# Weight sums of the odd blocks made in the last product's stage from raw weights, and a later place for one x group

## The chip, the cores and the metric

One core of one Trainium2 chip. The metric is the device time of one execution in microseconds (us); lower is better. The engines are named as in the profile: PE multiplies matrices (PEld is its weight load), DVE works elementwise with two inputs, ACT elementwise with one input and with activation functions, POOL and SP here mostly start DMAs. A chunk of a matrix is 128 wide.

## The reference, cut to what matters

```python
# x: 1 x 2048 x 640, w_gate and w_up: 640 x 1728, w_down: 1728 x 640
g = sigmoid((x * gate_w).sum(-1, keepdims=True))
a = dft_seq_re @ (x @ dft_hid_re.T) - dft_seq_im @ (x @ dft_hid_im.T)
b = (gelu(x @ w_gate) * (x @ w_up)) @ w_down
out = g * a + (1 - g) * b
```

All arrays are float32. 1728 is 13 chunks of 128 and 64 columns over.

## The kernel before, in words

**Number format.** Every float32 operand is split into a high part (line 80, a copy by ACT into the short type that PE reads fast) and a low part (line 83, raw minus high, by DVE). A product of two operands is three matmuls (lines 99 to 101): high by high, low by high, high by low. So every operand costs one ACT and one DVE instruction before PE may use it.

**Fewer products.** Blocks are multiplied two by two with the Winograd form of Strassen's scheme, seven block products in place of eight. It needs sums of blocks on both sides: for weights with blocks A11, A12, A21, A22 these are S1 = A21 + A22, S2 = S1 - A11, S3 = A11 - A21 and S4 = A12 - S2 (each with its own signs in the code).

**The stages, in time.** First products (to about 50 us). The gate and up stage, chunks f = 1 to 12, to about 335 us: `gate_up` for both halves of x, in which every second chunk from 3 on (kind 1) also has `together` and `together_up`, products shared by two chunks. Then the last product's stage, the product with w_down (about 335 to 502 us): 28 steps, `kseq`, 14 for each half tp. Then the C stage (the sequence transform, to about 895 us) and the last stage.

**What sets the order.** In the gate and up stage the order of PE, ACT, DVE and POOL is written out by hand (`in_order`, line 104). Side work stands in a list `fills`, each piece with an estimated cost, and is spread between the products of a chunk (line 1170); `left_work` is work for the leftover 64 columns, which is done either at once or where `spare` stands in the list of the next chunk's weights (line 236). `LEFT_AT` (line 690) says in which chunk which leftover work is entered; `store_left` (line 693) stores its results by SP at the start of the next chunk. In the last product's stage the order of ACT and DVE is written out (line 1277), that of SP and POOL is the tile framework's. In step i, `load_k(i + 3)` starts loads, `split_k(i + 2)` makes high and low parts, `late` does what is left over from an earlier step, and `step_k(i)` gives the products to PE.

**Buffers.** Nearly all tiles of 4 KB a partition share one pool of 46 slots, tag "s4" (line 63); a new tile waits until a slot is free. Tiles of 2 KB share 14 slots, tag "m".

**The steps of the last product.** For each half: steps (b = 0, k = 0 to 5) with the blocks A11, A12, e5 and S4; then the left block (b = 0, k = NK = 6), which joins the first chunk of w_down (`wd0`) with the 64 rows over (`wdr`); then (b = 1, k = 0), (b = 1, NK), which uses the left block's S2, S1, S3 and A22, and (b = 1, k = 1 to 5). So the left block is step 6 of the first half and step 20 of the second, and the step that uses its sums is 8 or 22. For each chunk k the weight sums are made beforehand in the gate and up stage and kept in DRAM as `wsd`; those of the left block are kept as `wsl`.

**sum_left (line 623).** In chunk 10 it loads A11 and A21 (`lw`), the narrow rows twice (`lm`) and the upper rows of the first chunk twice (`ld`), makes six sums on DVE (lines 637 to 645) and stores them into `wsl` (eight blocks, two stores). `load_k` for the left block then loads them beside the raw weights (lines 828 to 833), and `split_k` (lines 877 to 888) makes high and low parts of all blocks at once: `kc` and `ka` of the narrow ones, `kh` and `kl` of the wide ones.

**x groups (load_xn, line 757).** Eight groups of x for the C stage. Four of them are loaded, summed and split during the last product's stage, in the steps that `XN_AT` names: 1, 7, 18 and 24. A group takes seven slots, of which four stay until the end of the C stage.

**xq and xz.** In chunks of kind 1 after the third, POOL loads `xq` (line 1165), operands of `together`, and SP loads two `xz` tiles (line 746), whose row sums (line 750, DVE) make the gate g.

Of the kernel before, what the change touches and what calls it, by code (L numbers as in the profile page):

```python
# [22 lines left out]
NF = F // P  # L23
FR = F - NF * P
NK = (NF - 1) // 2
XN_AT = [1, 7, 18, 24]
GM_AT = [2, 17]
EORD = [0, 2, 1, 3, 4]
PAIRED = 3
# [6 lines left out]
def kernel(  # L36
# [27 lines left out]
    nc = tc.nc  # L64
# [14 lines left out]
    def high(hi, raw):  # L79
        nc.scalar.activation(hi, raw, AF.Copy)  # L80

    def low(hi, lo, raw):
        nc.vector.tensor_tensor(lo, raw, hi.bitcast(F32), op=ALU.subtract)  # L83

    def split(hi, lo, raw):
        high(hi, raw)
        low(hi, lo, raw)
# [37 lines left out]
    h0 = [dram.tile([P, 4, T], F32, tag=f"h0{p}", name=f"h0{p}") for p in range(2)]  # L125
    wsu, wneg = ([dram.tile([P, 8, P], F32, tag=f"{n}{p}", name=f"{n}{p}") for p in range(ND)] for n in ("wsu", "wneg"))
    uA, uT = ([[dram.tile([P, 4, T], F32, tag=f"u{n}{j}{p}", name=f"u{n}{j}{p}") for p in range(ND)] for j in range(2)] for n in "AT")
    grd, gmd = ([dram.tile([1, 2 * T], F32, tag=f"{n}{p}", name=f"{n}{p}") for p in range(2)] for n in ("grd", "gmd"))
    wsl = dram.tile([P, 8, P], F32, tag="wsl", name="wsl")
# [11 lines left out]
    def at(hilo, i):  # L141
        h, l = hilo
        return h[:, i], l[:, i]
# [6 lines left out]
    tt = nc.vector.tensor_tensor  # L150
# [82 lines left out]
    late_work, left_work, left_out = [], [], []  # L233
# [383 lines left out]

        return [(0, load), (84, do), (84, do)]

    def chunks(name):  # L620
        return mtile(F32, name).rearrange("p (b c) -> p b c", c=P)

    def sum_left():


        w, m, d = chunks("lw"), chunks("lm"), chunks("ld")
        nc.sync.dma_start(w, wd0[:, :4])
        for q in range(2):
            rows = slice(q * FR, (q + 1) * FR)
            nc.sync.dma_start(m[rows], wdr[:, :4])  # L630
            nc.sync.dma_start(d[rows], wd0[:FR, :4])
        a11, a21, a22 = w[:, 0:2], w[:, 2:4], m[:, 2:4]
        own = {}

        def first():
            s = own["s"] = chunks("ls")
            tt(s[:, 0:2], a21, a11, op=ALU.subtract)
            tt(a21[:FR], a21[:FR], a22[:FR], op=ALU.add)
            tt(m[:, 0:2], m[:, 0:2], a22, op=ALU.subtract)

        def second():
            s = own["s"]
            tt(a11, a11, a21, op=ALU.subtract)
            tt(d[:, 0:2], d[:, 0:2], d[:, 2:4], op=ALU.subtract)
            tt(s[:, 2:4], m[:, 0:2], d[:, 0:2], op=ALU.add)
            left_out.append((wsl[:, 0:4], w))
            left_out.append((wsl[:, 4:8], s))

        return [(100, first), (100, second)]

    def sum_h0(tp):


        f1, f2, b22 = (mtile(F32, f"lf{tp}{k}") for k in range(3))
        for v, k in ((f1, 0), (f2, 1), (b22, 3)):
            nc.sync.dma_start(v, h0[tp][:, k])

        def first():
            tt(f1, f2, f1, op=ALU.subtract)
            for k in (0, 2):  # L660
                rows = slice(FR if k else 0, P)
# [25 lines left out]

        return [(122, first), (61, second)]

    LEFT_AT = {2: lambda: [*sum_h0(0), *sum_h0(1)], 6: partial(sum_h0_narrow, 0), 10: sum_left, 11: lambda: [], 12: partial(sum_h0_narrow, 1)}  # L690


    def store_left():
# [120 lines left out]
    kraw, ktile = {}, {}  # L814

    def load_k(i):


        tp, b, k = kseq[i]
        n = f"{tp}{b}{k}"  # L820
        r = None
        if not (k == NK and b):
            r = slot(F32, [P, 8, P], f"kw{n}")
        if k == NK and b:
            src = hL[tp]
        elif k == NK:
            m = slot(F32, [P, 8, P], f"km{n}")
            nc.sync.dma_start(r[:, 0:2], wd0[:, 0:2])
            nc.sync.dma_start(r[:, 2:8], wsl[:, 0:6])
            for q in range(2):  # L830
                nc.sync.dma_start(m[q * FR : (q + 1) * FR, :5], wdr)
            nc.sync.dma_start(m[:, 5:7], wsl[:, 6:8])
            nc.sync.dma_start(m[:, 7], wd0[:, 4])
            r, src = (r, m), h0[tp]
        elif b:
            nc.sync.dma_start(r[:, 0:2], wd[k, :, 6:8])
# [33 lines left out]
    def split_k(i):  # L870
        tp, b, k = kseq[i]
        n = f"{tp}{b}{k}"
        r, raw = kraw.pop(i)
        if k == NK and b:
            W = ktile.pop(("left", tp))
        elif k == NK:
            r, m = r
            c, a = slot(F32R, [P, 8, P], f"kc{n}"), slot(F32R, [P, 8, P], f"ka{n}")
            high(c, m)
            high(a[:FR, :7], m[:FR, :7])  # L880
            low(c[FR:, :7], a[FR:, :7], m[FR:, :7])
            low(c[:, 7], a[:, 7], m[:, 7])
            h, l = slot(F32R, [P, 8, P], f"kh{n}"), slot(F32R, [P, 8, P], f"kl{n}")
            split(h, l, r)
            W = {name: (at((h, l), 2 * q), at((h, l), 2 * q + 1)) for q, name in enumerate(("A11", "S2", "S1", "S3"))}
            mx = {"A12": (a[:, 0], a[:, 1]), "A22": (a[:, 2], a[:, 3]), "e5": a[:, 4], "S4": (a[:, 5], a[:, 6])}
            W = W, (c[:, 7], a[:, 7]), mx
            ktile["left", tp] = W
        else:
            h, l = slot(F32R, [P, 8, P], f"kh{n}"), slot(F32R, [P, 8, P], f"kl{n}")  # L890
            split(h, l, r)
            names = ("A22", "S1", "S2", "S3") if b else ("A11", "A12", "e5", "S4")
            W = {name: (at((h, l), 2 * q), at((h, l), 2 * q + 1)) for q, name in enumerate(names)}
        B = []
        for q in range(2):
            v = hl(f"kb{n}{q}")
            split(*v, raw[q])
            B += [at(v, 0), at(v, 1)]
        ktile[i] = W, B

    kb = {"alone": False}
    after = []

    def late():
        for do in after:
            do()
        after.clear()
# [123 lines left out]
    with in_order(ACT, DVE, PE):  # L1031
# [5 lines left out]
        for d in range(ND):  # L1037
# [3 lines left out]
            if d == 0:  # L1041
                a, b = halves
# [56 lines left out]
        W, work = make_w(1)  # L1099
# [93 lines left out]
    with in_order(PE, ACT, DVE, POOL):  # L1193
        for f in range(1, NF):
# [80 lines left out]
            W = nxt  # L1275
# [5 lines left out]
    for i in range(len(kseq)):  # L1281
        if i + 3 < len(kseq):
            load_k(i + 3)
        if i + 2 < len(kseq):
            split_k(i + 2)
        late()
        if i in GM_AT:
            gm[GM_AT.index(i)] = gate_tile(gmd, GM_AT.index(i), f"gm{i}")
        if i in XN_AT:
            load_xn(XN_AT.index(i))  # L1290
        m = i - (len(kseq) - 3)
        if m >= 0:
# [12 lines left out]
        while todo:  # L1305
            todo.popleft()[1]()
# [50 lines left out]
    for i, (j, ri, b, sp) in enumerate(cseq):  # L1357
# [21 lines left out]
        if not b:  # L1379
# [17 lines left out]
            if lst:  # L1397
# [4 lines left out]
                for d in range(2):  # L1402
                    c = sv["c11", d]
# [5 lines left out]
        else:  # L1409
# [21 lines left out]
            if lst:  # L1431
                for d in range(2):
                    s2 = copy(X[d], f"s2{n}{d}")
                    a = mtile(F32, f"sa{n}{d}")
# [4 lines left out]
                for d in range(2):  # L1439
                    a, c21 = sv["a", d], mtile(F32, f"c21{n}{d}")  # L1440
# [3 lines left out]
                for d in range(2):  # L1444
                    s2, a, r, c12 = sv["s2", d], sv["a", d], sv["r", d], sv["c12", d]
# [41 lines left out]
    for i, (tp, b, p) in enumerate(useq[: 3 * ND]):  # L1487
        n = f"{tp}{b}"
        m = i - 2 * ND
# [20 lines left out]
        if not b:  # L1510
            for q in range(2):
                sv["c11", q] = copy(X[q], f"ys{n}{q}")
            for q in range(2):
                c = sv["c11", q]
# [3 lines left out]
            ls = [copy(L[t], f"yl{n}{t}") for t in range(2)]  # L1518
# [12 lines left out]
        for q in range(2):  # L1531
            s2, a = es[q]
# [159 lines left out]
```

## Time and profile before

| | |
|---|---|
| three runs | 1022.97 us median, 1022.27 to 1024.85 |
| profiled execution | 1022.46 us, of which the span from the first to the last instruction is 1020.5 |
| granted TensorE clock | 1.0 in every slice |
| DMA | 269.15 MB, 264 GB/s on average |

A view of waits has, in each row, the engine, the tile and line that waited, what it waited for, and the total, number and longest of these waits in us. A timeline row has start, duration, engine, line, operation, output <- inputs and shape, and in brackets the idle time before it and what seems to have ended it. "L83" is line 83, which may be a helper's. Where a wait is for several things, the row names the one that came last by the profile. Matmuls are pipelined: each is shown as 0.39 us long, although one starts every 0.23 us.

### The profile page before, as it was taken

Reading aid. Unit: us, or ns where it says so; the run is one execution under the profiler, and the core shown is the slowest. Engines: PE = TensorE matmul, PEld = TensorE weight load, DVE = VectorE, ACT = ScalarE, POOL = GpSimd, SP = SyncE. Lnnn points to the kernel's source line nnn. Section 1 sums busy time; section 2 is a strip of 40 time slices with the busy share of each in tenths; the row PEclk is TensorE's granted clock in tenths of the full one; section 3 lists DMA queues with packets and bytes.
Section 4 is the critical chain, followed back from the end, with each engine's and each line's share of the span. In section 5 each row is a group of like instructions: output and inputs, shape, how many; then the busy total and the mean of one; then the engine's idle time right before and its main releaser. Section 6 shows DMA issues by size and latency. Waiting matters only on the chain.

```text
span 1020.5 us, 13286 instructions
## 1 busy us (share of the span) xinstructions
PE 1015.2 (99%) x4483; PEld 839.0 (82%) x4483; DVE 823.9 (81%) x1163; ACT 485.9 (48%) x635; POOL 166.9 (16%) x295
## 2 busy tenths in 40 slices
PE   9999999999999999999999999999999999999998
PEld 7888888888878888888888888888888888888887
DVE  6987877877778979987898975898588859797796
ACT  6544534353535577366455343444344444465340
POOL 0121242323231200100011022102210200021112
PEclk9999999999999999999999999999999999999999
DMA  7468588968799999969776778658965877897855
GB/s 270 168 216 269 182 273 275 313 224 289 229 326 312 409 344 373 349 259 351 261 235 193 247 264 310 220 190 295 300 208 208 297 252 269 329 317 221 260 152 92
DMA packets 98084, 269.15 MB, mean 264 GB/s; under 512 B 12832, under 2 KB 28064, under 8 KB 98016
## 3 DMA queue, kind: packets, MB, share of 16 engines
q1 hardware_dynamic: 72096, 186.94, 53.6%
q0 software_dynamic: 25776, 81.30, 24.4%
q8 instruction: 35, 0.57, 0.2%
q14 instruction: 33, 0.27, 0.1%
q10 hardware_dynamic: 144, 0.07, 0.0%
HBM read 193.53 MB, written 70.80 MB: 259 GB/s over the span
## 4 chain that ended last, share of the span: by engine, by line
PE 98%; DMA 1%; DVE 1%; issue 0%; POOL 0%; SPq 0%; ACT 0%; POOLq 0%
PE pX L101 7%; PE pX L99 7%; PE pX L100 7%; PE pZ L101 4%; PE pZ L99 4%; PE pZ L100 4%; PE pL L101 3%; PE pL L99 3%; PE pL L100 3%; PE pV L101 2%; PE pV L99 2%; PE pV L100 2%; PE pY L101 1%; PE pR L101 1%; PE pQ L101 1%; PE pY L100 1%
## 5 line engine op out<-in xcount | busy, mean ns | idle before, releaser
L80 ACT ACTIVATE ch<-csa 128x1024 fp32r<-128x1024 f32 x32 | 34.0, 1064 | 89.5 <-DVE csa L797 70.6
L83 DVE TENSOR_TENSOR cl<-cra,ch 128x1024 fp32r<-128x1024 f32 x32 | 39.1, 1222 | 22.8 <-ACT ch L80 22.6
L80 ACT ACTIVATE ch<-cra 128x1024 fp32r<-128x1024 f32 x32 | 33.9, 1059 | 45.5 <-PE pL L100 15.6
L83 DVE TENSOR_TENSOR cl<-crb,ch 128x1024 fp32r<-128x1024 f32 x32 | 39.1, 1222 | 17.3 <-ACT ch L80 17.3
L100 PE MATMUL pL<-cl,xah 128*128 128x512 f32 x128 | 49.8, 389 | 0.0
L101 PE MATMUL pL<-ch,xal 128*128 128x512 f32 x128 | 49.8, 389 | 0.0
L99 PE MATMUL pL<-ch,xah 128*128 128x512 f32 x128 | 49.3, 389 | 0.0
L403 POOL DMA_DIRECT2D hA<-s x48 | 26.1, 544 | 131.5 <-DVE s L561 111.9
L80 ACT ACTIVATE ch<-crb 128x1024 fp32r<-128x1024 f32 x32 | 33.8, 1055 | 27.7 <-DVE cl L83 11.1
L83 DVE TENSOR_TENSOR cl<-csb,ch 128x1024 fp32r<-128x1024 f32 x32 | 39.2, 1224 | 4.5 <-ACT ch L80 2.3
L83 DVE TENSOR_TENSOR cl<-csa,ch 128x1024 fp32r<-128x1024 f32 x32 | 39.1, 1222 | 2.9 <-PE pR L100 1.7
L80 ACT ACTIVATE ch<-csb 128x1024 fp32r<-128x1024 f32 x32 | 34.0, 1062 | 12.5 <-PE pR L101 4.5
L555 ACT ACTIVATE s<-s 128x512 f32<-128x512 f32 x24 | 15.2, 634 | 47.0 <-DVE s L554 47.0
L83 DVE TENSOR_TENSOR kl<-kw,kh 128x1024 fp32r<-128x1024 f32 x26 | 31.7, 1220 | 6.9 <-ACT kh L80 6.9
L550 DVE TENSOR_TENSOR s<-s,pX 128x512 f32<-128x512 f32 x24 | 16.4, 684 | 19.8 <-PE pX L101 14.5
L1353 POOL DMA_DIRECT2D uA<-c x8 | 4.3, 540 | 169.8 <-DVE c L1441 169.6
L934 POOL DMA_DIRECT2D out<-ks x12 | 6.5, 542 | 154.2 <-DVE ks L933 153.6
L147 ACT ACTIVATE s<-pX 128x512 f32<-128x512 f32 x40 | 23.2, 597 | 15.5 <-PE pX L101 14.4
L403 POOL DMA_DIRECT2D hT<-s x48 | 26.0, 541 | 24.1 <-DVE s L578 8.1
L80 ACT ACTIVATE kh<-kw 128x1024 fp32r<-128x1024 f32 x26 | 27.2, 1048 | 2.0 <-DMA kw<-wsd 2.0
L100 PEld LDWEIGHTS pL<-cl,xah 128*128 128x128 f32 x128 | 24.0, 188 | 5.0
L101 PEld LDWEIGHTS pL<-ch,xal 128*128 128x128 f32 x128 | 24.0, 188 | 5.0
(3612 smaller groups left out, 3474.0 us busy)
## 6 DMA issues: line engine op xcount, KB each, us to landing
cra<-in_ct SPq DMA_DIRECT2D x64, 512.0 KB, 4.1
crb<-in_ct SPq DMA_DIRECT2D x64, 512.0 KB, 5.0
hA<-s POOLq DMA_DIRECT2D x48, 256.0 KB, 5.8
hT<-s POOLq DMA_DIRECT2D x48, 256.0 KB, 6.0
kr<-hA SPq DMA_DIRECT2D x24, 512.0 KB, 6.8
kr<-hT SPq DMA_DIRECT2D x24, 512.0 KB, 7.8
ux<-uA SPq DMA_DIRECT2D x24, 512.0 KB, 5.9
ux<-uT SPq DMA_DIRECT2D x16, 512.0 KB, 5.5
```

The lines of the kernel that those rows point to most:

```text
L80: nc.scalar.activation(hi, raw, AF.Copy)
L83: nc.vector.tensor_tensor(lo, raw, hi.bitcast(F32), op=ALU.subtract)
L99: nc.tensor.matmul(ps, lh, rh, start=first, stop=False, skip_group_check=True)
L100: nc.tensor.matmul(ps, lh, rl, start=False, stop=False, skip_group_check=True)
L101: nc.tensor.matmul(ps, ll, rh, start=False, stop=last, skip_group_check=True)
L147: nc.scalar.activation(m, src, AF.Copy)
L403: nc.gpsimd.dma_start(to[:, i], src)
L550: tt(s5, s5, X, op=ALU.add)
L555: nc.scalar.activation(s2, s2, AF.Gelu_apprx_tanh)
L934: nc.gpsimd.dma_start(acc4[:, t] if tp and e == 4 else out[2 * tp + t, e], src)
L1353: nc.gpsimd.dma_start(to[:, i], src)
```

## The change

`sum_left`, its helper `chunks`, the DRAM tile `wsl` and the entries 10 and 11 of `LEFT_AT` go. The left block's weights are now loaded raw in `load_k`, in both halves: `wd0` whole into `r`, the narrow rows `wdr` twice into `m`, and the upper rows of `wd0` twice into a new tile `d`. `split_k` makes the sums that the b = 0 step and the narrow products need (three on DVE), and splits only A11 and e5 of the wide blocks. A new function `split_left`, called one step later (steps 5 and 19) behind `split_k` and `late`, makes S2, S1 and S3 in place in `r` (three sums) and splits seven blocks at once. The tiles `r` and `m` live until then. The third x group moves from step 18 to step 21.

```diff
-XN_AT = [1, 7, 18, 24]
+XN_AT = [1, 7, 21, 24]
...
-    def sum_left():
...
-    LEFT_AT = {2: lambda: [*sum_h0(0), *sum_h0(1)], 6: partial(sum_h0_narrow, 0), 10: sum_left, 11: lambda: [], 12: partial(sum_h0_narrow, 1)}
+    LEFT_AT = {2: lambda: [*sum_h0(0), *sum_h0(1)], 6: partial(sum_h0_narrow, 0), 12: partial(sum_h0_narrow, 1)}
...
             m = slot(F32, [P, 8, P], f"km{n}")
-            nc.sync.dma_start(r[:, 0:2], wd0[:, 0:2])
-            nc.sync.dma_start(r[:, 2:8], wsl[:, 0:6])
+            d = slot(F32, [P, 8, P], f"kd{n}")
+            nc.sync.dma_start(r[:, :5], wd0)
             for q in range(2):
-                nc.sync.dma_start(m[q * FR : (q + 1) * FR, :5], wdr)
-            nc.sync.dma_start(m[:, 5:7], wsl[:, 6:8])
-            nc.sync.dma_start(m[:, 7], wd0[:, 4])
-            r, src = (r, m), h0[tp]
+                rows = slice(q * FR, (q + 1) * FR)
+                nc.sync.dma_start(m[rows, :5], wdr)
+                nc.sync.dma_start(d[rows, :4], wd0[:FR, :4])
+            r, src = (r, m, d), h0[tp]
...
-            r, m = r
+            r, m, d = r
+            tt(m[:, 5:7], m[:, 0:2], m[:, 2:4], op=ALU.subtract)
+            tt(d[:, 0:2], d[:, 0:2], d[:, 2:4], op=ALU.subtract)
+            tt(m[:, 5:7], m[:, 5:7], d[:, 0:2], op=ALU.add)
             c, a = slot(F32R, [P, 8, P], f"kc{n}"), slot(F32R, [P, 8, P], f"ka{n}")
-            high(c, m)
+            high(c[:, :7], m[:, :7])
             high(a[:FR, :7], m[:FR, :7])
             low(c[FR:, :7], a[FR:, :7], m[FR:, :7])
-            low(c[:, 7], a[:, 7], m[:, 7])
-            h, l = slot(F32R, [P, 8, P], f"kh{n}"), slot(F32R, [P, 8, P], f"kl{n}")
-            split(h, l, r)
-            W = {name: (at((h, l), 2 * q), at((h, l), 2 * q + 1)) for q, name in enumerate(("A11", "S2", "S1", "S3"))}
+            x = slot(F32R, [P, 8, P], f"kx{n}")
+            split(x[:, 0:2], x[:, 2:4], r[:, 0:2])
+            split(x[:, 4], x[:, 5], r[:, 4])
...
+    def split_left(tp):
+
+
+        r, m = kraw.pop(("left", tp))
+        a11, a21 = r[:, 0:2], r[:, 2:4]
+        tt(r[:, 5:7], a21, a11, op=ALU.subtract)
+        tt(a21[:FR], a21[:FR], m[:FR, 2:4], op=ALU.add)
+        tt(a11, a11, a21, op=ALU.subtract)
+        h, l = slot(F32R, [P, 8, P], f"ksh{tp}"), slot(F32R, [P, 8, P], f"ksl{tp}")
+        split(h[:, :7], l[:, :7], r[:, :7])
+        for name, c in (("S2", 0), ("S1", 2), ("S3", 5)):
+            ktile["left", tp][0][name] = at((h, l), c), at((h, l), c + 1)
...
         late()
+        if i in (5, 19):
+            split_left(i // 14)
```

More of the change, by code (lines that the diff above doesn't have):

```diff
@@ L128 @@
     grd, gmd = ([dram.tile([1, 2 * T], F32, tag=f"{n}{p}", name=f"{n}{p}") for p in range(2)] for n in ("grd", "gmd"))
-    wsl = dram.tile([P, 8, P], F32, tag="wsl", name="wsl")
     hL = [dram.tile([P, 4, T], F32, tag=f"hL{p}", name=f"hL{p}") for p in range(2)]
@@ L618, in sum_wd @@
         return [(0, load), (84, do), (84, do)]
-    def chunks(name):
-        return mtile(F32, name).rearrange("p (b c) -> p b c", c=P)
-    def sum_left():
[L626 to L649, printed above, removed]
     def sum_h0(tp):
@@ L876, in split_k @@
         elif k == NK:
-            r, m = r
+            r, m, d = r
+            tt(m[:, 5:7], m[:, 0:2], m[:, 2:4], op=ALU.subtract)
+            tt(d[:, 0:2], d[:, 0:2], d[:, 2:4], op=ALU.subtract)
+            tt(m[:, 5:7], m[:, 5:7], d[:, 0:2], op=ALU.add)
             c, a = slot(F32R, [P, 8, P], f"kc{n}"), slot(F32R, [P, 8, P], f"ka{n}")
-            high(c, m)
+            high(c[:, :7], m[:, :7])
             high(a[:FR, :7], m[:FR, :7])
             low(c[FR:, :7], a[FR:, :7], m[FR:, :7])
-            low(c[:, 7], a[:, 7], m[:, 7])
-            h, l = slot(F32R, [P, 8, P], f"kh{n}"), slot(F32R, [P, 8, P], f"kl{n}")
-            split(h, l, r)
-            W = {name: (at((h, l), 2 * q), at((h, l), 2 * q + 1)) for q, name in enumerate(("A11", "S2", "S1", "S3"))}
+            x = slot(F32R, [P, 8, P], f"kx{n}")
+            split(x[:, 0:2], x[:, 2:4], r[:, 0:2])
+            split(x[:, 4], x[:, 5], r[:, 4])
             mx = {"A12": (a[:, 0], a[:, 1]), "A22": (a[:, 2], a[:, 3]), "e5": a[:, 4], "S4": (a[:, 5], a[:, 6])}
-            W = W, (c[:, 7], a[:, 7]), mx
+            W = {"A11": [(x[:, q], x[:, 2 + q]) for q in range(2)]}, (x[:, 4], x[:, 5]), mx
+            kraw["left", tp] = r, m
             ktile["left", tp] = W
```

## The prediction

> **What bounds the kernel now.** I read the page first, then who waited for whom on PE, then the busy time by stage.
>
> ```profile
> span 1020.5 us, 13286 instructions
> PE 1015.2 (99%) x4483; PEld 839.0 (82%) x4483; DVE 823.9 (81%) x1163; ACT 485.9 (48%) x635; POOL 166.9 (16%) x295
> ...
> PE pH11t L99 <- DVE s L453: 0.7, 1, 0.7
> PE pH11t L99 <- DMA xq<-xp: 0.3, 1, 0.3
> ```
>
> PE is busy 1015.2 of 1020.5 us, and the change alters no product: the same matmuls run on other names. What it can gain is idle time of PE; what it can lose is a new idle time. The two waits shown are the only ones PE has after its first 6 us, and both fall in one place, chunk 11 of the gate and up stage. The loss there is read by comparing two equal stretches of PE's work. Each runs from the first "S1" product of an even chunk to that of the next even one:
>
> ```profile
> 223.02 0.39 PE L99 MATMUL pZ<-xT01h,ws8h 128*128 128x512 f32 x1
> 270.70 0.39 PE L99 MATMUL pZ<-xT01h,ws10h 128*128 128x512 f32 x1
> 319.95 0.39 PE L99 MATMUL pZ<-xT01h,ws12h 128*128 128x512 f32 x1
> ...
> 223.02:270.70 47.68, 47.68 (x212) 39.41 (x210) 36.03 (x71) 21.62 (x35) 13.73 (x25) 1.00 0.83 265
> 270.70:319.95 49.25, 48.32 (x211) 39.23 (x210) 37.37 (x75) 22.36 (x36) 13.76 (x25) 1.00 0.92 295
> ```
>
> (The columns of the last two rows: stretch, length, busy time of PE, weight load, DVE, ACT and POOL, granted clock, DMA share, GB/s.) Chunks 8 and 9 take 47.68 us with PE never idle; chunks 10 and 11, the same products, take 49.25. So **1.57 us** is lost here, and the DMA engines are busier (0.92 against 0.83). Nothing else in the span is worth as much.
>
> Where the 1.57 us sits:
>
> ```profile
> 288.88 0.39 PE L101 MATMUL pV11t<-x05h,wa11l 128*128 128x512 f32 x1
> 289.55 0.50 PE L99 MATMUL pH11t<-xq,wq11h 128*128 128x512 f32 x1 [0.28 <-DMA xq<-xp]
> 298.98 0.39 PE L101 MATMUL pZ<-x15h,wa11l 128*128 128x512 f32 x1
> 300.02 0.50 PE L99 MATMUL pH11t<-x121h,wq11h 128*128 128x512 f32 x1 [0.65 <-DVE s L453]
> 298.53 0.83 DVE L750 CUSTOM_DVE_ANT_0 xz<-xz,gwb 128x640 f32<-128x640 f32 x1 [5.16 <-DMA hT<-s]
> ```
>
> Matmuls follow each other every 0.227 us (47.68 over the 210 weight loads). From 288.88 to 289.55 is 0.67, so 0.44 too long; from 298.98 to 300.02 is 1.04, so 0.81 too long. The rest of the 1.57 is small delay behind these two. The first waits for xq, a load issued from POOL. The second waits for DVE, which is held, its order being fixed, by the row sum of xz (line 750): that could not start before xz had landed.
>
> **Why they land late, and what the removal does.**
>
> ```profile
> SPq L695 <- DVE ld L644: 12.0, 1, 12.0
> ...
> 277.64 0.33 SPq L695 DMA_DIRECT2D wsl<-lw  x1
> 278.44 0.33 SPq L695 DMA_DIRECT2D wsl<-ls  x1
> ...
> L95 POOL DMA_DIRECT2D wq11l<-wq11r x1: 862/862/862, 277.2 to 277.2; - x1
> DMA to landing us min/median/max: 6.4/6.4/6.4
> ...
> L95 POOL DMA_DIRECT2D wq9l<-wq9r x1: 865/865/865, 229.6 to 229.6; - x1
> DMA to landing us min/median/max: 4.1/4.1/4.1
> ...
> 284.02 1.24 POOL L1165 DMA_DIRECT2D xq<-xp  x2 [4.95 <-DVE s L554]
> 287.23 1.49 SPq L746 DMA_DIRECT2D xz<-in_xz  x2
> DMA to landing us min/median/max: 11.1/11.7/12.3
> DMA to landing us min/median/max: 6.6/7.0/7.4
> ```
>
> The stores of the sums (wsl, 256 KB each by their shape) are issued at 277.64 and 278.44, right after the accumulating load of wq11l from POOL. That load takes 6.4 us to land; its twin two chunks earlier, wq9l, takes 4.1. Two of the three xq loads go out only at 284.02, just after wq11l has landed (277.2 plus 6.4 is 283.6), although the view names DVE as the last event. So they collide with the next weights, and the xz loads issued at 287.23 take 11.1 to 12.3 us (first of the last two rows), where those of chunk 9 take 6.6 to 7.4. Besides, SP stands 12.0 us in front of the first wsl store, and the small weight loads behind it go out late, into the same crowd. Both parts of the loss thus hang on sum_left's DMAs. The removal takes five loads (768 KB by shape) and two stores (512 KB) out of these two chunks, 1.3 MB; the difference between the two stretches is about 1.9 MB (49.25 us by 295 GB/s less 47.68 by 265).
>
> By the Trainium skill (DMA: Bandwidth & Descriptors, "Issuing engines are not separate DMA queues") transfers begun by SP and by POOL end on the same sixteen engines and interleave. The trace agrees: SP's stores and POOL's wq11l stretch together. By that rule the 1.3 MB weigh on xq and xz whichever queue carries them, and the gain would be the whole 1.57.
>
> The DVE work that leaves:
>
> ```profile
> 276.08 0.42 DVE L637 TENSOR_TENSOR ls<-lw 128x256 f32<-128x256 f32 x1
> 277.99 0.42 DVE L645 TENSOR_TENSOR ls<-lm,ld 128x256 f32<-128x256 f32 x1
> ```
>
> First and last of six; together 276.08 to 278.41, 2.3 us. DVE stands idle 5.16 us before the xz sum that matters (row above), so its work is not what is late there, and I count these at nothing; were they the cause, the gain would still lie inside the 1.57. Bounds of the removal: 0 to 1.57. I take **1.4**, near the upper end, since chunks 8 and 9 show the same stage without these DMAs and without loss. The little I hold back is for two loads of ua that chunk 11 has beside them and chunk 9 has not.
>
> **What is added in the last product's stage,** once in each half (tp 0 and 1):
>
> ```profile
> L83 DVE TENSOR_TENSOR ka<-km,kc 64x896 fp32r<-64x896 f32 x2 | 2.2, 1090 | 0.3 <-ACT kc L80 0.2
> 363.93 0.94 ACT L80 ACTIVATE ka<-km 64x896 fp32r<-64x896 f32 x1
> ```
>
> In split_k of the left block: three more sums at 0.42 (1.26); the low part of eight blocks (1.22, a row below) becomes one of two blocks (0.42, priced as a 256-wide sum); the one-block low part stays. Net DVE +0.46. In split_left: three sums (1.26) and a seven-block low part (1.09), 2.35. DVE gains **2.8 us** a half; ACT gains a 0.94 high part and loses about 0.45, so 0.5. SP issues five DMAs a half where it issued six, with 0.13 MB less to move by shape. Raw weights and sums hold one to three slots of the 46 longer.
>
> The cover in the first half is the idle time that DVE has two steps on:
>
> ```profile
> 378.46 1.28 DVE L974 TENSOR_TENSOR ks<-ks,kV 128x512 f32<-128x512 f32 x2 [2.64 <-PE kV L947]
> 382.93 1.23 DVE L83 TENSOR_TENSOR kl<-kw,kh 128x1024 fp32r<-128x1024 f32 x1 [3.19 <-ACT kh L80]
> ```
>
> 2.64 and 3.19 us, both ended by PE's own progress (the second through ACT's copies of the L banks), so 2.8 us are absorbed and step 9 starts as before. Queued behind split_left on both engines are first the operands of step 8, which PE takes three steps later. Cost nothing; without that cover at most 2.8. In the second half the group moved away from step 18 leaves 4.7 us of room just there.
>
> **What is moved.** The third x group goes from step 18 to step 21, the twin of step 7, where the second group already stands. The twin shows the price:
>
> ```profile
> 388.75 0.95 DVE L83 TENSOR_TENSOR xal<-xn,xah 128x768 fp32r<-128x768 f32 x1
> 393.44 1.23 DVE L83 TENSOR_TENSOR kl<-kw,kh 128x1024 fp32r<-128x1024 f32 x1
> 394.58 1.22 DVE L83 TENSOR_TENSOR kb0120l<-kr,kb0120h 128x1024 fp32r<-128x1024 f32 x1
> 397.02 0.62 PE L99 MATMUL kX<-kb0120h,kh 128*128 128x512 f32 x2
> ...
> 473.75 1.21 DVE L83 TENSOR_TENSOR kb1120l<-kr,kb1120h 128x1024 fp32r<-128x1024 f32 x1
> 480.88 0.39 PE L99 MATMUL kX<-kb1120h,kh 128*128 128x512 f32 x1
> ```
>
> The group holds DVE 4.69 us (388.75 to 393.44). In the first half step 10's first operand is then done at 395.80, and PE takes it at 397.02: **1.2 us** to spare, and PE did not wait. In the second half it is now done at 474.96; plus 4.69 is 479.65 against 480.88, again 1.2 to spare. So nothing is lost as long as xn has landed:
>
> ```profile
> 461.66 0.38 SPq L836 DMA_DIRECT2D kw<-in_wd  x1
> 469.06 0.33 SPq L836 DMA_DIRECT2D kw<-in_wd  x1
> ...
> DMA to landing us min/median/max: 6.1/6.1/6.1
> ```
>
> At 461.66 the load that follows step 24's goes out today; xn's two loads now stand in that place. The twin's xn (the last row) landed after 6.1, so about 467.8; DVE wants it at 472.6. About 5 us of slack, and 1.2 behind it.
>
> **Sum.** Against the profiled execution (1022.46, its span of 1020.5 and 2.0 around it): minus 1.4, plus 0, is 1021.06. The median of the three runs is 1022.97, half a microsecond higher; with the same 1.4 it becomes 1021.57, and I forecast **1021.6**.
>
> **Rivals.** *No gain.* The ua loads or another slot order keep xq or xz late, so the change does not do there what it removes: 1022.6 to 1023.2, say 1023.0. For it: the ua loads are there in chunk 11 and not in 9. Against it: they are 256 KB beside 512 KB of stores, and go out earlier once SP no longer stands 12 us.
>
> *Slower, by xn in its new place.* With seven slots asked for at step 21 while the left block still holds its own, SP may have to wait for the release that today lets the next load out at 469.06. Then xn lands at 475.2, its high part takes 0.85, and the group starts at 476.0, not 472.6: 3.4 late, of which 1.2 are spare, so PE stands 2.2 us: 1023.8. It decides from 2 us beyond the forecast landing plus what DVE waits. One release later (5.4 us on) the loss is 7.6: 1029.2. Against it: until step 21 the four kept tiles of that group are free, more than the left block adds.
>
> **How the numbers follow.** Forecast (0.8 to 1.57 gained, nothing lost; from the lowest run, 1022.27 less 1.57, to the median less 0.8: 1020.7 to 1022.2): 0.66. No gain: 0.14. xn late by one release: 0.12. Late by two, or a wait I have not found: 0.08. The range 1020.7 to 1024.0 holds these three cases (0.92), less the scatter at their ends, and leaves out the last. A measurement of this kernel tells about 0.3% from no change: faster means under 1019.9, which the rows do not allow (0.01); slower means over 1026.04, only the last case (0.07); within is 0.92.
>
> **What would show it.** Right: no wait of PE on pH11t; chunks 10 and 11 in about 47.7 us; wq11l landing in 4 to 5 us; step 24 with about 1 us to spare. Wrong: a PE wait on a kb or kl name after step 21, or one in the first half at steps 8 to 10, or xz still landing after 11 us.

## The result, and the profile after

The changed kernel takes **1022.55 us** (median of 21 runs, 1021.20 to 1024.42), the kernel before in the same comparison 1023.51 (21 runs, 1022.27 to 1027.39): ratio 0.9987, 95% interval 0.9981 to 0.9993. The gain is 0.96 us by the medians, below the 0.3% that the prediction called distinguishable, but with an interval that leaves out one. The forecast was 1021.6 with a gain of 1.4; the time lies inside the range given.

The profiled execution took 1021.4 us. First its page:

```profile
span 1019.4 us, 13282 instructions
PE 1014.7 (100%) x4483; PEld 839.1 (82%) x4483; DVE 826.9 (81%) x1171; ACT 485.4 (48%) x639; POOL 166.8 (16%) x295
```

DVE has eight instructions and 3 us more than before, and the span is 1.1 us shorter: the work added stands beside PE. What PE still waits for, in the view of waits of after:

```profile
PE idle L1019 <- PEq L1666: 0.8, 1, 0.8
PE pm L1050 <- ACT x011h L80: 0.5, 1, 0.5
```

Both stand at the very start. The two waits on pH11t are gone. The two stretches of two chunks each, cut at the same products as in the prediction (stretch, length, busy time of PE, weight load, DVE, ACT and POOL, clock, DMA share, GB/s):

```profile
223.48:271.16 47.68, 47.68 (x212) 39.42 (x211) 36.05 (x71) 21.62 (x35) 13.74 (x25) 1.00 0.79 254
271.16:318.85 47.69, 47.69 (x212) 39.41 (x210) 35.29 (x69) 22.53 (x36) 13.76 (x25) 1.00 0.91 288
```

Chunks 10 and 11 now take 47.69, so all of the 1.57 us came back in this execution. Length by rate gives the bytes: 13.73 MB here against 14.53 before, and 12.11 against 12.64 in chunks 8 and 9; together 1.33 MB less, as the shapes said (part of sum_left's loads went out before chunk 10 began). But the DMA share of chunks 10 and 11 hardly fell, from 0.92 to 0.91. A mean share over 48 us is not what decides. The timeline of after shows what does:

```profile
289.30 0.39 PE L101 MATMUL pV11t<-x05h,wa11l 128*128 128x512 f32 x1
289.53 0.39 PE L99 MATMUL pH11t<-xq,wq11h 128*128 128x512 f32 x1
298.82 0.39 PE L101 MATMUL pZ<-x15h,wa11l 128*128 128x512 f32 x1
299.05 0.39 PE L99 MATMUL pH11t<-x121h,wq11h 128*128 128x512 f32 x1
296.35 0.83 DVE L718 CUSTOM_DVE_ANT_0 xz<-xz,gwb 128x640 f32<-128x640 f32 x1 [2.52 <-DMA hA<-s]
282.81 1.24 POOL L1149 DMA_DIRECT2D xq<-xp  x2 [3.26 <-DMA wq11l<-wq11r]
263.62 0.43 SPq L674 DMA_DIRECT2D ua<-in_wu  x1
280.25 0.33 SPq L674 DMA_DIRECT2D ua<-in_wu  x1
```

Both products on pH11t follow their forerunner after 0.23. The row sum of xz starts 25.19 us after the stretch begins (296.35 less 271.16), where before it was 27.83. The xq loads go out 11.65 us into it (282.81), no longer 13.32, as soon as wq11l has landed by this row, and one ua load leaves SP at 263.62, no longer behind the stores. The landing times behind that, in the views of single tiles (wq11l, then xz between 280 and 302):

```profile
L95 POOL DMA_DIRECT2D wq11l<-wq11r x1: 862/862/862, 277.7 to 277.7; - x1
DMA to landing us min/median/max: 4.7/4.7/4.7
```

```profile
L714 SPq DMA_DIRECT2D xz<-in_xz x2: 327/328/328, 287.7 to 288.8; - x2
DMA to landing us min/median/max: 8.5/8.9/9.3
```

wq11l lands in 4.7 us (6.4 before), xz in 8.5 to 9.3 (11.1 to 12.3 before).

The other place the prediction watched is step 24 of the last product's stage, timeline of after:

```profile
477.35 1.22 DVE L83 TENSOR_TENSOR kb1120l<-kr,kb1120h 128x1024 fp32r<-128x1024 f32 x1
479.78 0.62 PE L99 MATMUL kX<-kb1120h,kh 128*128 128x512 f32 x2
480.92 0.39 PE L100 MATMUL kX<-kb1120l,kh 128*128 128x512 f32 x1
```

kb1120l ends at 478.57; PE begins the step at 479.78, 1.21 later, as forecast. (PE needs the low part only at 480.92; e6 below turns on that.)

### The profile page after: what moved, and what is told of

It is laid out like the page before. It is cut to its first block, busy times and chain, and to the rows that moved or that the text cites. A ratio compares the mean times of both kernels' runs of the same rounds, so it can differ in the third digit from the quotient of the medians.

```text
span 1019.4 us, 13282 instructions
## 1 busy us (share of the span) xinstructions
PE 1014.7 (100%) x4483; PEld 839.1 (82%) x4483; DVE 826.9 (81%) x1171; ACT 485.4 (48%) x639; POOL 166.8 (16%) x295
## 4 chain that ended last, share of the span: by engine, by line
PE 99%; DMA 0%; SPq 0%; ACT 0%; DVE 0%; issue 0%
PE pX L100 7%; PE pX L101 7%; PE pX L99 7%; PE pZ L100 5%; PE pZ L101 5%; PE pZ L99 5%; PE pL L100 3%; PE pL L99 3%; PE pL L101 3%; PE pV L100 2%; PE pV L99 2%; PE pV L101 2%; PE pY L100 1%; PE pY L99 1%; PE pR L100 1%; PE pR L99 1%
## 5 line engine op out<-in xcount | busy, mean ns | idle before, releaser
L402 POOL DMA_DIRECT2D hA<-s x48 | 26.1, 544 | 133.5 <-DVE s L560 113.9
L83 DVE TENSOR_TENSOR kl<-kw,kh 128x1024 fp32r<-128x1024 f32 x24 | 29.3, 1222 | 5.7 <-ACT kh L80 5.7
L99 PEld LDWEIGHTS pL<-ch,xah 128*128 128x128 f32 x128 | 24.0, 188 | 5.0
```

What stands on the lines that cost most here:

```text
L99: nc.tensor.matmul(ps, lh, rh, start=first, stop=False, skip_group_check=True)
L402: nc.gpsimd.dma_start(to[:, i], src)
```

## The experiments

Theory at the outset: the 1.57 us in chunks 10 and 11 come from sum_left's DMAs, and the moved x group costs nothing. Twelve runs were made, in three groups, each group on one chip beside the kernel before (e11 is the changed kernel over again). Times are medians; "loss in chunks 10 and 11" is their stretch less 47.68 in the profiled execution. DVE's idle sums named below have results that nothing uses.

### e2: sum_left two chunks earlier (in before)

```diff
-    LEFT_AT = {..., 10: sum_left, 11: lambda: [], 12: ...}
+    LEFT_AT = {..., 8: sum_left, 12: ...}
```

> The kernel before, with the whole of sum_left (loads, sums, stores) entered two chunks earlier, in chunk 8 in place of 10. Theory: the loss moves with it: the stretch of chunks 8 and 9 grows from 47.68 us to 48.5 to 49.3 with PE waiting on pH9t, and that of chunks 10 and 11 falls to 47.7; the time stays within 0.5 us of before. Rival (chunk 11 is late for its own reasons, with the ua loads): the loss stays in 10 and 11.

Measured: 1021.40 us (10 runs; before 1022.76), ratio 0.9987, 0.9977 to 0.9997. No PE wait in any stage, no loss in chunks 10 and 11, and none in chunks 8 and 9 either: the loss did not move with the work, it went. The xz loads of chunk 9 in that kernel, and the row sum of chunk 11:

```profile
L746 SPq DMA_DIRECT2D xz<-in_xz x2: 327/327/327, 240.1 to 242.8; - x2
DMA to landing us min/median/max: 7.8/8.2/8.6
```

```profile
297.25 0.83 DVE L750 CUSTOM_DVE_ANT_0 xz<-xz,gwb 128x640 f32<-128x640 f32 x1 [3.38 <-DMA xz<-in_xz]
```

So neither the theory nor the rival came true. In chunk 9 the landing is 7.8 to 8.6, where before has 6.6 to 7.4. That this is the stores' doing is not shown: in e5, which has nothing of sum_left in chunks 8 and 9, the same loads took 7.9 to 8.7. There is room for it in any case. So sum_left is not dear by itself; its **place** was. Chunk 11, which has the ua loads as well, stands near its limit without it. The same gain as the change gives is had without adding anything to the last product's stage.

### e1: the stores started by ACT (in before)

```diff
-            left_out.append((wsl[:, 0:4], w))
-            left_out.append((wsl[:, 4:8], s))
+            nc.scalar.dma_start(wsl[:, 0:4], w)
+            nc.scalar.dma_start(wsl[:, 4:8], s)
```

> The kernel before, but the two stores of the left block's weight sums are started by ACT right behind the sums, not by SP, which then no longer stands in front of them. Theory (the stores' own 512 KB stretch the accumulating load of wq11l and, through xq, what follows): the stores are in flight at the same time as before, so chunks 10 and 11 still take 48.5 to 49.3 us and wq11l lands 6 us or more after its start. Rival (SP standing 12 us in front of the first store pushes the small loads into the crowd): 47.7 to 48.0 us, wq11l in under 5 us, and about 1.3 us less than before. Second rival (the six sums on DVE): 49.25 as before.

Measured: 1022.04 us (10 runs; before 1022.76), ratio 0.9986, 0.9977 to 0.9996. The profiled execution (1022.46, among the higher of the ten) still has a loss of 1.38, nearly all in one wait now; views of waits, timeline and the xz tile:

```profile
PE pH11t L99 <- DVE s L453: 1.1, 1, 1.1
```

```profile
278.29 0.33 ACTq L646 DMA_DIRECT2D wsl<-lw  x1
278.86 0.33 ACTq L647 DMA_DIRECT2D wsl<-ls  x1
298.75 0.82 DVE L750 CUSTOM_DVE_ANT_0 xz<-xz,gwb 128x640 f32<-128x640 f32 x1 [4.96 <-DMA hT<-s]
```

```profile
L746 SPq DMA_DIRECT2D xz<-in_xz x2: 328/328/328, 287.6 to 288.8; - x2
DMA to landing us min/median/max: 10.9/11.5/12.0
```

The stretch of 49.06 us is the theory's; wq11l landed in 5.5 us, which fits neither the theory (6 or more) nor the rival (under 5). PE no longer waits for xq, the part on xz stays: another issuing engine doesn't shorten the landing of xz. That agrees with the rule of the Trainium skill that the prediction weighed (DMA: Bandwidth & Descriptors, "Issuing engines are not separate DMA queues"). The timed median is lower than this profile would suggest, so the loss isn't the same in every execution.

### e3 and e7: DVE's sums alone, then with two stores (in after)

```diff
+    def six_sums():   # six sums of 256 columns in chunk 10, as sum_left's
...
+    LEFT_AT = {10: six_sums, ...}
# e7 also, behind the last sum:
+                left_out.append((dsl[:, 0], s[0]))
+                left_out.append((dsl[:, 1], s[1]))
```

> The kernel after, with six sums of 256 columns put back on DVE in chunk 10 at the place of the old ones, on data that lie there anyway, without any load or store; their results are used nowhere. Theory: chunks 10 and 11 stay at 47.7 us and the time is that of after (1.3 us under before). Rival (DVE's 2.3 us were the cause): 48.5 to 49.3 us, the time of before.

> The kernel after, with the same six sums in chunk 10 and two stores of 256 KB of their results by SP, as the kernel before had them, but none of the five loads; the stored sums are used nowhere. Theory (the stores): the loss returns, chunks 10 and 11 take 48.3 to 49.3 us, PE waits on pH11t. Rival (the 768 KB of loads at 262 to 265 us): 47.7 us. Rival (SP's stand): returns as well, told from the theory by the run with the stores on ACT.

Measured, e3: 1021.54 us (10 runs; before 1022.76), ratio 0.9985, 0.9975 to 0.9995; no PE wait but the first, xz lands in 7.1 to 7.9. **DVE's sums are not the cause**; this term was rightly priced at nothing.

e7: 1023.02 (10 runs), ratio 1.0005, 0.9993 to 1.0018, 1.5 us over e3 on the same chip. But its profiled execution (1022.68) has a loss of only 0.02 in chunks 10 and 11; it lost 0.79 before chunk 10, most of it in chunk 7, and 0.58 in the C stage. The waits, and the DMA share between 280 and 284 (same columns as above):

```profile
PE pH7u L99 <- DMA xu<-xv: 0.4, 1, 0.4
```

```profile
280.00:284.00 4.00, 4.00 (x19) 3.32 (x18) 2.71 (x4) 1.79 (x4) 0.40 (x1) 1.00 1.03 253
```

The DMA engines are full there (before 1.01, after 0.86), and yet xz landed in 9.3 to 10.2, in time. So the two stores cost something in the timed runs, but the profiled execution does not show it where it was looked for. Which of sum_left's seven DMAs does most is not settled. For all seven together, in chunk 10, the rows agree: with them the first xz landed in 9.7 to 11.3 us (before, e1, e5, e8), with none of them in chunk 10 in 7.1 to 9.6 (nine executions), and with the two stores alone, here, in 9.3.

### e8 and e9: the row sum of xz later (in before, in after)

```diff
-                k = len(fills) // 2
+                k = len(fills) * (3 if f == 11 else 2) // 4
```

The first row sum of chunk 11 then stands six DVE instructions later.

> The kernel before, with one edit: in chunk 11 the first row sum of xz stands six DVE instructions later, behind lines 245 to 248 and 453 to 459, so that line 453, for which PE waits, no longer stands behind it. Theory as it now stands (the stores are only harmful because they make xz land later than the 10.4 us that DVE's order leaves it): xz still lands after 10.5 to 12 us, PE's wait for line 453 is gone, what is left in chunks 10 and 11 is the xq part, up to 0.6 us (48.3 at most), and the time falls by 0.8 to 1.0. Rival (another engine is late in chunk 11 too): a new PE wait takes its place and the stretch stays near 49.

> The kernel after with the same later row sum in chunk 11. Theory: in the profiled execution of after nothing is left to gain in chunks 10 and 11 (47.7 us); if the half of its executions that take 1.2 us longer lose it at this wait, the median falls by up to 1 us under that of after; if they lose it elsewhere, it is that of after, 1.3 us under before.

Measured, e8: 1022.59 (10 runs; before 1022.39), ratio 1.0003, 0.9994 to 1.0012. e9: 1021.54, ratio 0.9991, 0.9982 to 1.0001. The waits of e8's execution in the gate and up stage:

```profile
PE pH11t L99 <- DMA xq<-xp: 0.4, 1, 0.4
```

As the theory wanted: the part that hung on the row sum is gone (f = 11's half of the stretch is 23.88, undisturbed), the part that hung on xq stays (0.72 in the stretch). So the loss has two causes, and both are landing times. They do not simply add up: in before the half of the stretch with xq loses 0.62 and the other 0.95, but in e1, where PE doesn't wait for xq, the row sum alone costs 1.38, since PE comes to it earlier. The 0.8 to 1.0 us that were expected of the time did not come. In the profiled execution a start 0.95 us later than before's takes up the 0.85 gained; why the median of ten runs gains nothing is not shown. (The expectation gave xz 10.4 us to land; by the table below it is about 9.6.)

In e9 0.8 us were lost between steps 0 and 24 of the last product's stage (0.28, 0.13 and 0.39 in steps 0 to 6, 7 to 13 and 14 to 23). The view of waits names none of it, but the timeline shows where the first 0.41 sits, at the end of step 6 and in step 7:

```profile
376.71 0.95 ACT L80 ACTIVATE ksh<-kw 128x896 fp32r<-128x896 f32 x1 [3.34 <-DVE kw L879]
379.47 1.06 ACT L146 ACTIVATE ks<-kX 128x512 f32<-128x512 f32 x2
380.10 0.50 PE L99 MATMUL kX<-kb0100h,kh 128*128 128x512 f32 x1
```

ACT stands 3.34 us until the last sum of `split_left` (line 879) is done, then makes its high part `ksh`, and only behind that the copies of `kX`, the bank that PE needs next. In after ACT stands as long, but the first copy ends 2.2 us before PE starts step 7. In e9 the same chain runs 2.4 us later, counted from the first S1 product of chunk 12, and PE is late. What made DVE late there, and the 0.39 near step 15, stay open.

### The limit, from eleven executions

The row sum's start, counted from the first S1 product of chunk 10, beside the loss in chunks 10 and 11 (kernels with the row sum at its usual place; us):

| kernel | first xz lands in | row sum starts | loss |
|---|---|---|---|
| e3 | 7.1 | 23.82 | 0.02 |
| e11 | 7.9 | 24.54 | 0.01 |
| after | 8.5 | 25.19 | 0.01 |
| e12 | 8.6 | 25.23 | 0.01 |
| e7 | 9.3 | 26.01 | 0.02 |
| e2 | 9.4 | 26.05 | 0.00 |
| e4 | 9.5 | 26.17 | 0.30, behind xu |
| e6 | 9.6 | 26.27 | 0.26, behind xu |
| e5 | 9.7 | 26.41 | 0.97, most of it behind a 0.6 wait on xq |
| e1 | 10.9 | 27.64 | 1.38 |
| before | 11.1 | 27.83 | 1.57 |

In e4 and e6 the row sum is not what costs: no product on pH11t is late there. What is late comes 37 us into the stretch, behind a load of xu from POOL. In e4:

```profile
302.15 1.18 POOL L1149 DMA_DIRECT2D xu<-xv  x2 [4.41 <-DMA hT<-s]
307.78 0.39 PE L101 MATMUL pX<-xT03h,ws11l 128*128 128x512 f32 x1
308.12 0.50 PE L99 MATMUL pH11u<-xu,wu11h 128*128 128x512 f32 x1
```

The first of these two loads landed after 5.9 us, so at 308.1 (after: 5.0), and 307.78 to 308.12 is 0.34 in place of 0.23; the rest of the 0.30 is small delay behind it. So the row sum costs nothing up to 26.27, and at 27.64 and 27.83 the loss is the start less 26.26. In every one the row sum starts 0.16 us behind the landing of the first xz, also where the row names another DMA (hT, hA) as what ended DVE's idle time. Without sum_left the landing still varies from 7.1 to 9.6, so these kernels stand from 2.4 us under the limit to right at it, and the landing of xu is a third one whose room can run out.

### e5 and e4: the move alone, and all but the move

e5 is before, e4 is after, with one line changed:

```diff
# e5, in before
-XN_AT = [1, 7, 18, 24]
+XN_AT = [1, 7, 21, 24]
# e4, in after
-XN_AT = [1, 7, 21, 24]
+XN_AT = [1, 7, 18, 24]
```

> The kernel before with only the move of the third x group from step 18 to 21. Theory: the loss in chunks 10 and 11 stays (48.5 to 49.3 us in the profiled execution), no new PE wait, the first operand of step 24 ready 1.2 us before PE takes it; the time is that of before within 0.4 us. Rival (xn lands late in its new place): a PE wait at step 24 of 1 to 3 us.

> The kernel after with the third x group back at step 18. Theory: the move is no part of the gain: chunks 10 and 11 at 47.7 us, no PE wait in the last product's stage, the time of after; the first operand of step 24 is ready 5 us or more before PE takes it (1.2 in after), that of step 21 some 4 to 7 us. Rival (with the group at 18 the left block's longer life uses up the slots and a load waits): a PE wait at steps 20 to 23, 1 to 5 us slower.

Measured, both beside before at 1022.39: e5 1022.75 (10 runs), ratio 1.0006, 0.9997 to 1.0016; e4 **1021.14** (10 runs, nine of them up to 1021.61), ratio 0.9988, 0.9979 to 0.9998, the lowest median of all. The whole gain comes from the removal, and the move, if anything, takes some back. In e5's profile step 24 has its 1.22 us to spare and PE doesn't wait there. But the C stage, from its first product to the first of the last stage, took 392.08 us, where before, after and e4 take 391.68. That was a cost in a place where nobody had looked, and e11, e6, e12 and e10 were made for it.

### e11: the changed kernel again

> The kernel after, unchanged, to stand on the same chip beside the one with the group at 18. Theory (the fourth x group ends later with the third at step 21, and its room in the first C steps is about half a microsecond): chunks 10 and 11 in 47.7 us, the C stage 391.68 to 392.3 us, and a ratio to before of 0.9985 to 0.9992, at or slightly above that of the group at 18. Rival (the placing doesn't matter): the two medians within 0.2 us and the C stage 391.68 in both.

Measured: 1022.46 us (11 runs; before 1022.90), ratio 0.9992, 0.9983 to 1.0001. The same code as after, and its profiled execution lost 0.98 us in the C stage. First the C stage in after, then in e11 (columns as above):

```profile
501.54:893.22 391.68, 391.68 (x1729) 324.32 (x1728) 311.43 (x390) 170.63 (x200) 48.67 (x90) 1.00 0.75 255
```

```profile
501.27:893.93 392.66, 392.42 (x1729) 323.86 (x1728) 312.55 (x392) 170.56 (x200) 48.68 (x90) 1.00 0.74 255
```

The same products, longer by 0.98, of which the waits name only 0.24 (`pX` on `ch`, at 522); the rest is small delay in the matmuls around it. What is late there is the x group that DVE makes in the first C steps. Its last sum in e11, and the group before it, made in step 24, with the load that it waited for:

```profile
491.40 0.96 DVE L83 TENSOR_TENSOR xbl<-xs,xbh 128x768 fp32r<-128x768 f32 x1 [0.28 <-ACT xbh L80]
510.52 0.96 DVE L83 TENSOR_TENSOR xbl<-xs,xbh 128x768 fp32r<-128x768 f32 x1 [0.28 <-ACT xbh L80]
522.07 0.73 PE L99 MATMUL pX<-ch,xah 128*128 128x512 f32 x2 [0.24 <-ACT ch L80]
```

```profile
L734 SPq DMA_DIRECT2D xn<-in_xn x1: 333/333/333, 479.5 to 479.5; - x1
L80 ACT ACTIVATE xah<-xn x1: 846/846/846, 486.8 to 486.8; 128x768 fp32r<-128x768 f32 x1
DMA to landing us min/median/max: 7.2/7.2/7.2
```

And the same load in e4, where the third group is at step 18, with what SP and DVE do next:

```profile
478.71 0.33 SPq L734 DMA_DIRECT2D xn<-in_xn  x1
485.74 0.33 SPq L756 DMA_DIRECT2D cra<-in_ct  x1
489.20 0.96 DVE L83 TENSOR_TENSOR xbl<-xs,xbh 128x768 fp32r<-128x768 f32 x1 [0.28 <-ACT xbh L80]
499.40 0.69 DVE L967 TENSOR_TENSOR ksa<-ks,kQ 128x512 f32<-128x512 f32 x1 [1.22 <-ACT ks L146]
509.62 0.96 DVE L83 TENSOR_TENSOR xbl<-xs,xbh 128x768 fp32r<-128x768 f32 x1 [0.28 <-ACT xbh L80]
```

Counted from the first C product (501.86 in e4, 501.27 in e11), xn goes out at -23.15 in e4 and at -21.80 in e11: 1.35 later. In all six executions with the group at 21 and no idle sums it is -21.8, in all with the group at 18 -23.15. In e4 SP's next loads (cra) follow at 485.74, when xn has landed after 5.8 us. In e11 the first of them leave at 481.72 and 482.86, and xn takes 7.2. That these loads stretch it is not shown: with the group at 21 and no idle sums xn took 5.9 to 7.2, and only 6.0 in after beside the same loads; with the group at 18 it took 5.6 to 6.0 in six executions, but 7.0 in e12. So the fourth group ends at -8.91 in e11, at -11.70 in e4. DVE's idle 1.22 us (last but one row) takes up part; in e11 there is none there. The remainder reaches the fifth group, which ends 8.72 us into the C stage in e4 and 10.21 in e11.

By an estimate from the fit in the Trainium skill (DMA: Bandwidth & Descriptors, "Anatomy of one DMA — SWDGE (gpsimd) path": 2.0 us and the bytes at 436 GB/s; made for loads started by POOL, these start from SP) the 384 KB of xn would land in 2.9 us. The rows have 5.4 to 7.2; in after it is 6.0, at a DMA share of 1.04 while it is under way. The next group's xn, of the same size, landed in 3.05 there at a share of 0.76, near the estimate. So the estimate fits that row and not the ones in the full stream; there the measurement decides.

### e6 and e12: how much room there is

```diff
# e6, in after, behind the third x group
+        if i == 21:
+            for k in range(5):
+                tt(mtile(F32, f"dx{k}"), gwb[:, 0:512], gwb[:, 128:640], op=ALU.subtract)
# e12, in e4, behind the fourth x group
+        if i == 24:
+            for k in range(4):
+                tt(mtile(F32, f"dx{k}"), gwb[:, 0:512], gwb[:, 128:640], op=ALU.subtract)
```

> The kernel after, with five DVE sums of 512 columns (about 0.6 us each by the estimate from the 256-column sums at 0.42, so about 3.0 us) behind the third x group at step 21, their results unused. It measures the room that the prediction counted at step 24. Theory (the room is the 1.21 us that the trace of after shows between kb1120l and PE): PE waits 3.0 less 1.21, 1.8 us, on a kb or kl name at step 24, and the span is 1.8 to 3.0 us longer than after's. Rival (DVE has more room, since it catches up later): no wait of PE, and a span like after's.

> The kernel after, with the third x group back at step 18, and four DVE sums of 512 columns (about 2.4 us) behind the fourth group at step 24, their results unused. It measures how late the fourth group may be. Theory (1.22 us of DVE's idle time behind the group take up a part, and about 0.5 us of room in the first C steps another): the C stage is 2.4 less 1.22 less 0.5, about 0.7 us longer (0.4 to 1.0) than 391.68, in small halts of PE on the pX products of the first C steps, with no PE wait in the last product's stage. Rival (the halts in the C stage of the runs with the group at 21 have another cause): no loss there, or the whole 2.4.

Measured, e6: 1023.77 us (11 runs; before 1022.90), ratio 1.0009, 1.0000 to 1.0018: 1.31 over e11. Its waits, and the timeline at step 24:

```profile
PE kX L100 <- DVE kb1120l L83: 0.5, 1, 0.5
PE pX L99 <- ACT ch L80: 0.4, 1, 0.4
PE pZ L99 <- DVE ks L976: 0.2, 1, 0.2
```

```profile
480.15 1.23 DVE L83 TENSOR_TENSOR kb1120l<-kr,kb1120h 128x1024 fp32r<-128x1024 f32 x1
481.44 0.50 PE L100 MATMUL kX<-kb1120l,kh 128*128 128x512 f32 x1 [0.47 <-DVE kb1120l L83]
```

The wait is 0.47, not 1.8, and the stage 0.79 longer. kb1120l was late by 2.9 us against PE; the room was 2.35: 1.21 to the start of the step, and 1.14 more (480.92 less 479.78 in after), since step 24 begins with five products that need only high parts. 2.9 less 2.35 is 0.57, near the measured. The other 1.62 us were lost in the C stage.

e12: 1023.13 (11 runs), ratio 1.0005, 0.9996 to 1.0014; waits of its C stage:

```profile
PE pX L99 <- ACT ch L80: 0.4, 1, 0.4
PE pZ L99 <- DVE ks L976: 0.2, 1, 0.2
```

The loss is in the C stage, as expected, but it is 1.65 and not 0.7: xn took 7.0 us in this execution where e4 had 5.8, so the group was 1.2 late before the idle sums began. (The profiled 1024.77 also holds a start 1.8 us later than after's.)

The end of the fifth group, in us after the first C product, beside what the C stage took over 391.68, for every kernel that was run:

| kernel | third group at | fourth ends | fifth ends | C stage over 391.68 |
|---|---|---|---|---|
| before, e1, e2, e4, e8, e10 | 18 | -11.5 to -11.85 | 8.72 | 0.00 |
| e3 | 21 | -10.29 | 8.83 | 0.00 |
| after | 21 | -10.13 | 9.00 | 0.00 |
| e5 | 21 | -9.50 | 9.62 | 0.40 |
| e9 | 21 | -9.43 | 9.70 | 0.47 |
| e7 | 21 | -9.34 | 9.79 | 0.58 |
| e11 | 21 | -8.91 | 10.21 | 0.98 |
| e6 | 21, and sums | -8.28 | 10.84 | 1.62 |
| e12 | 18, and sums at 24 | -10.54 | 10.91 | 1.65 |

The loss is the fifth group's end less 9.23, to within 0.03, in all six kernels that lose anything, and nothing below. So the C stage has **0.5 us of room** (9.23 less 8.72), and a delay isn't made up in its first steps: one x group and two low parts there fill DVE for the whole step, 6.96 us from one xal to the next in after and 6.97 in e11. e12 reaches the same line with the group at 18, so it is the lateness that costs, not the move as such. In the six executions with the group at 21 and no idle sums, the fifth group's end is the landing time of the fourth group's xn plus 3.0 us (6.0 and 9.00 in after, 7.2 and 10.21 in e11). Nothing is lost there while xn lands within 6.2 us, so the loss comes and goes with one landing; the move has taken 1.35 us of that landing's room.

### e10: the candidate

e4 with e9's later row sum in chunk 11.

> The kernel after, with the third x group back at step 18 and the first row sum of chunk 11 six DVE instructions later. The candidate for the best of both. Theory (the removal is the whole gain, the move brings only risk): chunks 10 and 11 in 47.7 us, no PE wait on pH11t, the C stage 391.68 us from its first ch,xah product to its first yX product, and a time like that of the kernel with the group at 18, 1.2 to 1.5 us under before's on the same chip. Rival (the move helps somewhere): a time above that of the unchanged kernel after in this same call.

Measured: 1021.62 us (11 runs; before 1022.90), ratio 0.9989, 0.9980 to 0.9998; C stage 391.68, chunks 10 and 11 in 47.70. Below e11 in the same group by 0.84, but the runs overlap (1021.19 to 1023.33 against 1021.50 to 1024.25). Not better than e4: the later row sum bought nothing that can be seen, and its profiled execution lost 1.0 us in chunks 5 and 7 (0.40 and 0.60); xz of chunk 7 took 9.3 to 10.1 us to land there (7.7 to 8.1 in after). That is the next place of the same kind.

## Why the prediction was right or wrong, point by point

**The loss and its cause: right.** 1.57 us in chunk 11, two parts, on xq and on xz, both landing times. After's windows, waits and landings came out as the prediction said they would; e8 separated the two parts in its profile, though its time did not fall; e3 cleared DVE; e1 cleared SP as the issuer of the stores. Right in kind, not in full: the prediction laid the loss to sum_left's DMAs and not to their place, and e2 showed them free two chunks earlier. Its 0.44 and 0.81 are the two long intervals alone; the halves of the stretch lose 0.62 and 0.95, and the whole 1.57 is set by the row sum's start. And what decides is landing times against fixed places in the order, of xz above all (26.1 us into the stretch), not the DMA share that it pointed to, which stayed at 0.91.

**The size of the gain from the removal, 1.4: right to about 0.1.** Against before on the same chip the three kernels that take the load off chunk 10 and keep the group at 18 gain 1.25 (e4), 1.28 (e10) and 1.36 (e2).

**The sums added in the last product's stage, 0: right.** In after and e4 no stage shows a wait in either half, and from the first S1 product of chunk 12 to the first C product before, after and e4 all take 182.69 us. It is not nothing in every execution: in e9 0.41 us were lost at step 7. The prediction priced the instructions on ACT, but not that ACT stands in front of the high part until DVE's sums are done, with PE's next bank behind it.

**The moved group, 0: the step that failed.** The prediction said that nothing is lost as long as xn has landed, and looked at the first operand of step 24. Both numbers it gave there came true or better (1.21 us to spare; 2.35 by what PE really needs). But it counted the moved group's room only up to the next step. It didn't follow SP's queue on to the next group, whose load goes out 1.35 us later, nor DVE's order on into the C stage, where half a microsecond is all the room. By pairs on one chip, group at 21 against group at 18: e3 and e2 0.14 (e3 has six idle sums), e5 and before 0.36, e9 and e4 0.40 (e9 with the later row sum), e11 and e10 0.84 (e10 with it). Each is within the scatter, all have one sign; in the six profiled executions with the group at 21 and no idle sums in that stage the C stage lost 0.00, 0.00, 0.40, 0.47, 0.58 and 0.98. The price is thus 0 to 1 us, execution by execution, which is the size of the difference between the 1.4 forecast and the 0.96 measured (0.44 in e11's group too). That it is the whole of it is not shown: single executions also lost 0.3 at xu (e4, e6) and 0.8 in the last product's stage (e9).

**The base.** The forecast stood on a median of three runs, 1022.97; in the 21 runs before has 1023.51, and 1022.39 to 1022.90 in the three later groups. Of the 0.98 us between 1021.57 and 1022.55, 0.54 is this and 0.44 the smaller gain.

**The rivals.** No gain: refuted by after's windows. xn late at step 21: it wasn't; PE had no wait at step 24. The prediction's picture of that rival, an x group made late by SP's order and handed on through DVE, is what happened, one group further on, at 0 to 1 us where the rival had 2.2.

## What to carry to other kernels

Count a moved load's room not to the first consumer alone but along its queue and its engine's fixed order, until an idle gap has taken the delay up; here the gap was 1.2 us and the room behind it 0.5, and the loss came in the next stage. Where a stage runs at the edge of a landing time, moving the bytes to a chunk with room is worth as much as removing them. And a loss that depends on a landing is there in some executions and not in others: look at the room in several profiles before calling it nothing.

## What the runs showed of the hardware

- One load, same size, same place in the order, lands in times that differ by 2 us and more between executions and variants of this kernel: the first xz of chunk 11 (320 KB) 7.1 to 9.6 without sum_left in chunk 10, and 9.3 to 11.3 with its stores there, xn of the fourth group (384 KB) 5.4 to 7.2.
- Small waits spread: a named wait of 0.24 on pX stood for 0.98 us of lost time, a named 0.47 at step 24 for 0.79. A stretch between two equal products measures the loss; the view of waits gives its place.
- The start differs too: the first S1 product of chunk 1 came between 52.59 and 53.54 us in thirteen of the fourteen profiled executions, and at 54.88 in one. A single profiled time can't tell kernels apart here by less than a microsecond; the stretches can.
